# Every softmax from a copied score tile, the weights' clamp on GpSimd, and a planner with new costs for TensorE's forms

## The chip, the cores and the metric

The kernel runs on one core of a Trainium2 chip. The metric is the device time of one launch in microseconds, the median of several runs. Five engines share the work and run in their own order: PE (TensorE), DVE (VectorE), ACT (ScalarE), POOL (GpSimd) and SP, which issues the transfers.

## The reference, cut to what matters

Eight batches of attention (8 heads, 576 positions, head size 64) feed a mixing layer. In the attention a score counts only if it lies within tau of its row's largest:

```
scores = scale * q @ k.T
thresh = max(scores) - tau
attn = exp(where(scores >= thresh, scores, -1e9) - max(scores))
attn = attn / (sum(attn) + 1e-9)
x = attn @ v                       # heads side by side: 576 x 512 per batch
theta = x @ w_theta
y = w_tok_r @ (x * cos(theta)) + w_tok_i @ (x * sin(theta))
u = x + y
out = u + maximum(u @ w_ch, 0)
```

## The kernel before

**Precision.** fp32 products are made of three products of a high and a low part (names with 1 and 2, h and l). The weights are split once, in `convert`: four pieces of w_theta, nine of w_tok and four of w_ch, 17 in all. Each piece is loaded, passes ACT (absolute value, L407) and five DVE instructions (clamp L411, shift L418, then L425, L432, L436), ACT again, and three kinds of matmul on PE (L455 to L457).

**Attention.** Heads go in 32 pairs, four to a batch. A pair has five units: four of 128 query rows for both heads, and one for the last 64 rows of both together. So a pair has nine softmaxes of 128 x 576, called heads below and counted from the program's start (heads 1 to 9 are pair 1). A unit's scores (L552) fill a tile of four PSUM banks (two for the last unit) that always starts at bank 0 for the full units: one score tile is in flight at a time, and the next unit's scores wait until all readers of the last are done. Two ways of making the softmax stand in `unit`, chosen by `n < AT["pp"]`:
- *direct*: one DVE reduction over both heads (L567), the limits (L592), Exp on ACT from PSUM (L614), and a mask by DVE that reads the scores in PSUM again (L621);
- *copied*: for each head DVE copies the negated scores to SBUF and takes the extreme on the way (L583), then the limits (L600), Exp from the copy (L631), and a mask that reads the copy and the Exp, both in SBUF (L638).

Then PE turns the head round in blocks of 128 x 128 (L654, and L681 for the last keys), ACT copies the blocks to `a` (L660), and PE multiplies by the values (L710). A pair's row sums are turned on PE (L726), inverted on DVE (L731, L734), sent through DRAM to be spread, and multiplied in (L745). Before, the first five pairs (45 heads) are direct and the other 27 pairs copied.

**Mixing.** Each batch's `mixture` (L791 with w_theta or w_ch, L903 to turn, L932 with w_tok) is laid between the attention units of the next batch; batch 8's attention is the last, and the end of the program is mixing alone.

**TensorE's forms.** Scores of the full units use the array as two halves of 64 rows (64*128 in the rows below), the value products as two halves of 64 columns (128*64), everything else, transposes too, the whole array (128*128).

**The order.** `Plan.run` decides it before the program is built: a list scheduler with a cost for each operation (`c_ps`, `c_two`, `c_fast`, `c_pool`), due times (the table `AT`), and a lock that keeps some DVE and POOL operations apart. What it decides is then the fixed order of each engine. Its only knowledge of the forms is 0.1 added where they differ.

Of the kernel before, what the change touches and what calls it, by code (L numbers as in the profile page):

```python
# [32 lines left out]
AT = {  # L33
    "wait": 0.046, "margin": 0.0, "held": 1.639, "theta": 3.43, "theta_by": 2.2, "tok": 17.5, "tok_by": 0.87, "ch": 54.39,
    "ch_by": 3.55, "q": -4.49, "k": -10.75, "raw": -1.58, "v": -4.5, "m0": 8.15, "m1": 4.1, "score": -2.04, "nm": 0.6,
    "add": -4.86, "exp": -2.35, "mask": -0.34, "wrap": -0.65, "turn": 0.32, "copy": 1.0, "last": 0.06, "v0": 4.11, "v1": 13.27,
    "vcopy": -0.32, "div": 6.28, "rows": -1.77, "dmul": 0.16, "x": 0.95, "x_by": 0.51, "wm": -9.49, "ev": 2.19, "zst": 0.37,
    "sin": -0.88, "zm": -0.69, "zh": 0.09, "zl": -2.61, "y": -0.99, "u": 1.64, "fa": 0.68, "fa_by": 1.07, "ft": 0.17,
    "ft_by": 0.05, "pq": 28, "px": 2, "pu": 0, "pz": 6, "pk": 1, "ta": 4, "cut": 2, "pp": 5, "vm": 0, "m6": 0.15, "wp": 0,
    "wq": 0, "ua": 2, "ord": 0, "hang": 0, "n_rawq": 2, "n_rawk": 2, "n_q": 4, "n_rb": 2, "n_ang": 2, "n_xh": 4, "n_xl": 4,  # L40
    "n_wm": 3, "n_z": 3, "n_k": 4, "n_s2": 3, "n_nm": 4, "n_sc": 4, "n_a0": 1, "n_a1": 1, "n_zh4": 4, "n_zl4": 4, "n_zh1": 2,
    "n_zl1": 2, "n_xT": 7, "n_v": 2, "n_rows": 2, "n_rt": 1, "keep": -3.37,
}


# [61 lines left out]
class Plan:  # L107
# [39 lines left out]
    def run(self):  # L147
# [51 lines left out]
        while todo:  # L199
# [50 lines left out]
def tile_attn_moe(  # L250
# [11 lines left out]
    nc = tc.nc  # L262
# [118 lines left out]
    def convert(src, n, raw_cls, places, key, done, turn):  # L381
# [12 lines left out]
        def hb():  # L394
            return raw()[:, :n, 1]
# [13 lines left out]
        dve(
            c_fast(n),  # L410
            lambda: nc.vector.tensor_scalar(  # L411
                out=mb().bitcast(F32), in0=mb().bitcast(F32), scalar1=W_LEAST, scalar2=W_MOST, op0=ALU.max, op1=ALU.min
            ),
            key, (mag,), (mag,), lock=True,
        )
        dve(
# [118 lines left out]
    def unit(n, i):  # L535
# [69 lines left out]
        for j in heads:  # L605
# [5 lines left out]
            if n < AT["pp"]:  # L611
# [15 lines left out]
            else:  # L627
# [93 lines left out]
    def divide(n, key):  # L721
# [36 lines left out]
    def mixture(b, k0, k1):  # L758
# [134 lines left out]
        def flip(m, keys):  # L893
            z = zs[m]
            out = []
            for (c0, nb), key in zip(((0, 4), (4, 1), (5, 4)), keys):
# [8 lines left out]
                def tv(tp=tp, nb=nb):  # L905
# [181 lines left out]
```

## Time and profile before

| | |
|---|---|
| median of 3 runs | 1035.54 us (1034.57 to 1036.29) |
| the profiled execution | 1035.99 us, its span 1034.2 us |
| TensorE's mean granted clock | 0.992 |
| busy share of the span | PE 96%, DVE 77%, ACT 67%, POOL 23% |

The span is what the trace covers; 1.8 us lie around it. PE's share is an average of a first part of some 160 us, in which it often waits, and the rest, in which it hardly does. Busy times of matmuls overlap their neighbours'; how fast PE goes is read from the distance between starts.

### The profile page before, as it was taken

The page shows a single profiled execution, that of the slowest core. Times are in us where ns is not written, and L with a number is a line of the kernel's source. Part 1 is how long each engine was busy: PE and PEld are TensorE (multiplying, and loading weights), DVE is VectorE, ACT ScalarE, POOL GpSimd, SP SyncE. Part 2 cuts the span into 40 slices and gives each one's busy share as a digit, 9 for nine tenths or more (in the row PEclk, how much of TensorE's full clock was granted, in tenths as well). Part 3 has the DMA queues.
Part 4 walks back from the last instruction along what each step waited for, and adds up shares of the span by engine and source line. Part 5 has one row for each costly group of instructions (what it writes and reads, how often), then busy time and mean ns, then how long its engine had stood idle before and what let it go on. Part 6 is the DMA issues. An engine that isn't in the chain of part 4 may idle for free.

```text
span 1034.2 us, 21024 instructions
## 1 busy us (share of the span) xinstructions
PE 995.1 (96%) x8008; PEld 853.7 (83%) x8008; DVE 797.8 (77%) x1869; ACT 690.8 (67%) x1326; POOL 233.8 (23%) x257
## 2 busy tenths in 40 slices
PE   5888889999999999999999999999999999999998
PEld 3566578789898888898888888988888898888998
DVE  6998569987868778777877777887787869887462
ACT  6878577756786468765787558775687647864350
POOL 1002133111261123411252023511242112100100
PEclk9999899999999999999999999999999999999999
DMA  7651132234421143213430152212431142200601
GB/s 254 204 193 50 49 107 73 82 132 134 123 90 46 51 142 110 71 39 112 134 106 26 40 166 92 88 50 70 137 126 37 45 138 97 65 15 13 189 30 67
DMA packets 52308, 98.04 MB, mean 95 GB/s; under 512 B 12752, under 2 KB 21488, under 8 KB 52208
## 3 DMA queue, kind: packets, MB, share of 16 engines
q1 hardware_dynamic: 52208, 96.71, 29.1%
q8 instruction: 63, 1.03, 0.4%
q14 instruction: 37, 0.30, 0.1%
HBM read 82.90 MB, written 13.78 MB: 93 GB/s over the span
## 4 chain that ended last, share of the span: by engine, by line
PE 87%; DVE 6%; ACT 5%; issue 1%; DMA 1%; SPq 0%; ACTq 0%; DVEq 0%
PE banks_ps__66 L932 21%; PE banks_ps__66 L791 19%; PE banks_ps__66 L710 16%; PE banks_ps__66 L552 14%; PE banks_ps__66 L654 12%; PE banks_ps__66 L903 2%; PE banks_ps__66 L681 1%; DVE s L621 1%; DVE nm L567 1%; PE banks_ps__66 L455 1%; ACT a L660 1%; DVE zl L912 1%; DVE sc L583 1%; DMA z<-in_w_tok_dram 1%; PE banks_ps__66 L726 1%
## 5 line engine op out<-in xcount | busy, mean ns | idle before, releaser
L631 ACT ACTIVATE s<-sc,nm 128x576 f32<-128x576 f32 x243 | 186.5, 780 | 83.7 <-DVE sc L583 83.0
L638 DVE SCALAR_TENSOR_TENSOR s<-sc,nm,s 128x576 f32<-128x576 f32 x243 | 204.5, 869 | 39.0 <-ACT s L631 31.6
L583 DVE TENSOR_SCALAR_CACHE_REDUCE sc<-banks_ps__66 128x576 f32<-128x576 f32 x243 | 177.5, 746 | 66.2 <-PE banks_ps__66 L552 65.8
L660 ACT COPY a<-banks_ps__66 128x512 f32<-128x512 f32 x256 | 150.2, 591 | 94.0 <-PE banks_ps__66 L654 92.9
L654 PE MATMUL banks_ps__66<-ident,s 128*128 128x128 f32 x1152 | 173.4, 279 | 13.8 <-DVE s L621 12.9
L552 PE MATMUL banks_ps__66<-k,q 64*128 64x288 f32 (+1 forms) x1728 | 170.2, 311 | 7.7 <-ACT q L509 7.7
L710 PE MATMUL banks_ps__66<-a,v 128*64 128x320 f32 (+1 forms) x1280 | 171.8, 417 | 2.9 <-ACT a L668 1.7
L791 PE MATMUL banks_ps__66<-xh,wm 128*128 128x288 f32 x1024 | 171.6, 302 | 0.0
L932 PE MATMUL banks_ps__66<-wt_h,zh 128*128 128x288 f32 x576 | 166.1, 309 | 1.8 <-DVE zl L912 1.5
L654 PEld LDWEIGHTS banks_ps__66<-ident,s 128*128 128x128 f32 x1152 | 134.5, 142 | 40.2 <-DVE s L621 16.3
L368 POOL TENSOR_TENSOR k<-rawk,k 128x320 fp32r<-128x320 f32 x64 | 60.8, 972 | 460.5 <-issue 255.1
L932 PE MATMUL banks_ps__66<-wt_l,zh 128*128 128x288 f32 x576 | 162.4, 302 | 0.0
L552 PEld LDWEIGHTS banks_ps__66<-k,q 64*128 64x128 f32 (+1 forms) x1728 | 135.1, 188 | 32.0 <-issue 19.6
L791 PEld LDWEIGHTS banks_ps__66<-xh,wm 128*128 128x128 f32 x1024 | 144.8, 189 | 3.2 <-issue 2.2
L710 PEld LDWEIGHTS banks_ps__66<-a,v 128*64 128x64 f32 x1280 | 89.0, 139 | 67.4 <-issue 11.1
L932 PEld LDWEIGHTS banks_ps__66<-wt_h,zh 128*128 128x128 f32 x576 | 108.4, 188 | 4.9 <-DVE zl L912 3.2
L932 PEld LDWEIGHTS banks_ps__66<-wt_l,zh 128*128 128x128 f32 x576 | 108.6, 189 | 0.5 <-issue 0.5
L878 POOL TENSOR_TENSOR z<-z,xT 128x288 f32<-128x288 f32 x96 | 83.0, 905 | 94.5 <-ACT z L859 94.5
L791 PE MATMUL banks_ps__66<-xl,wm 128*128 128x288 f32 x512 | 98.3, 307 | 0.0
L932 PE MATMUL banks_ps__66<-wt_h,zl 128*128 128x288 f32 x576 | 97.5, 301 | 0.0
L932 PEld LDWEIGHTS banks_ps__66<-wt_h,zl 128*128 128x128 f32 x576 | 81.8, 188 | 2.2 <-issue 1.6
L791 PEld LDWEIGHTS banks_ps__66<-xl,wm 128*128 128x128 f32 x512 | 75.0, 189 | 2.0 <-issue 2.0
(79 smaller groups left out, 1249.3 us busy)
## 6 DMA issues: line engine op xcount, KB each, us to landing
wm<-wm_dram SPq DMA_DIRECT2D x64, 512.0 KB, 3.1
rawk<-in_kT_dram SPq DMA_DIRECT2D x32, 320.0 KB, 2.9
rawq<-in_qT_dram SPq DMA_DIRECT2D x32, 320.0 KB, 2.9
out_dram<-xT SPq DMA_DIRECT2D x31, 288.0 KB, 4.0
v<-in_vp_dram SPq DMA_DIRECT2D x32, 256.0 KB, 2.6
z<-in_w_tok_dram SPq DMA_DIRECT2D x9, 576.0 KB, 4.7
rb<-sums_dram SPq DMA_DIRECT2D x32, 144.0 KB, 3.1
wm_dram<-rb SPq DMA_DIRECT2D x16, 256.0 KB, 2.9
```

Of the source, the lines that this page charges most:

```text
L368: eng.tensor_tensor(out=out()[:, c0:c1], in0=in0()[:, c0:c1], in1=in1()[:, c0:c1], op=ALU.subtract)
L552: nc.tensor.matmul(ps()[:, 2 * j + h, :HS], q[a]()[r, i * P : (i + 1) * P], k[c]()[r, k0 : k0 + HS], start=(x == 0), stop=(x == 2))
L583: lambda j=j, sv=sv, sc=sc: nc.vector.tensor_scalar(out=view(sc()), in0=sv(), scalar1=-1.0, scalar2=None, op0=ALU.mult, op1=ALU.min, accum ...
L631: lambda j=j, sc=sc: nc.scalar.activation(out=s()[:, j], in_=sc(), func=AF.Exp, bias=nm()[:, j : j + 1], scale=-1.0),
L638: lambda j=j, sc=sc, total=total: nc.vector.scalar_tensor_tensor(out=s()[:, j], in0=sc(), scalar=nm()[:, 2 + j : 3 + j], in1=s()[:, j], op ...
L654: nc.tensor.transpose(out=tp()[:, c * P : (c + 1) * P], in_=s()[:, j, k0 : k0 + P], identity=ident)
L660: lambda j=j, tp=tp: nc.scalar.copy(out=a()[:, j:8:2, q0 : q0 + P], in_=tp().rearrange("p (c q) -> p c q", c=4)),
L710: nc.tensor.matmul(o()[64 * j : 64 * j + 64, :w], st, mv, start=(c == 0), stop=(c == 4))
L791: nc.tensor.matmul(ps[h]()[:, :HS], wm()[:, a, c, :], parts[c][bb]()[:, h * HS : (h + 1) * HS], start=first and n == 0, stop=final and n = ...
L878: eng.tensor_tensor(out=zi, in0=zi, in1=x[m]()[:, c0:c1], op=ALU.mult)
L903: nc.tensor.transpose(out=tp()[:, i * P : (i + 1) * P], in_=z()[:, c : c + P], identity=ident)
L932: nc.tensor.matmul(ps()[:, :HS], zz[c][lo]()[:, zz[c][2]], w[:, c, hs], start=(q + n == 0), stop=(q + n == len(work) - 1),)
```

## The change

- `pp` goes from 5 to 0: all 288 softmaxes take the copied way.
- The clamp of the first 13 weight pieces (`wc`: 13; w_theta and w_tok) goes from DVE to POOL, in two halves. The shift on DVE then waits for POOL.
- `SWITCH` gives the planner a cost for each pair of forms, with whole-array matmuls and transposes told apart; `favour` and `linger` make it pick, among PE's operations that are ready, one that is like the form in hand.
- The planner's costs of DVE's and POOL's operations are new (most DVE ones lower), and the due times in `AT` are another set.

No other arithmetic changes; the same 288 softmaxes, products and transfers are made.

```diff
-    "ft_by": 0.05, "pq": 28, "px": 2, "pu": 0, "pz": 6, "pk": 1, "ta": 4, "cut": 2, "pp": 5, "vm": 0, "m6": 0.15, "wp": 0,
+    "ft_by": 0.06, "pq": 28, "px": 2, "pu": 0, "pz": 6, "pk": 1, "ta": 4, "cut": 2, "pp": 0, "vm": 0, "m6": -0.89, "wp": 0,
...
+    "t_s": -0.13, "m_s": 1.51, "wc": 13,
...
+def SWITCH(old, new):
+    if old is None or (old in "mt" and new in "mt") or old == new:
+        return 0.0
+    if new == "t":
+        return 0.15
+    if old in "rv" and new in "rv":
+        return 0.145 if new == "v" else 0.196
+    return 0.198
...
+        def favour(o):
+            if o.mode == "v":
+                return AT["v_r"] if mode == "r" else AT["v_m"]
+            if mode not in ("r", "v") or o.mode == mode:
+                return 0.0
+            return AT["t_s"] if o.mode == "t" else AT["m_s"]
...
+            if e == PE:
+                t0 += AT["linger"]
+                return min(((o.key + favour(o), o.n), t, o) for t, o in got if t <= t0)[1:]
...
             if e == PE:
-                form = o.mode if o.mode in "vr" else "m"
-                if mode is not None and mode != form:
-                    occ += 0.1
-                mode = form
+                occ += SWITCH(mode, o.mode)
+                mode = o.mode
...
+        if turn < AT["wc"]:
+            for i in range(2):
+                gps(
+                    c_pool(n // 2), lambda i=i: clamp(nc.gpsimd, slice(n * i // 2, n * (i + 1) // 2)), key, ((mag, i),),
+                    ((mag, i),),
+                )
+        else:
+            dve(c_fast(n), lambda: clamp(nc.vector), key, (mag,), ((mag, [0, 1]),), lock=True)
```

What the planner makes of it is seen in the orders. First DVE in pair 4 (the fourth of the first batch), two units. Before (L567 reduction, L592 limits, L621 masks, L745 the row sums multiplied in, L368 a low part):

```order
L567 TENSOR_REDUCE nm<-banks_ps__66 128x2
L592 TENSOR_SCALAR nm<-nm,small 128x2
L621 SCALAR_TENSOR_TENSOR s_1027,rows<-banks_ps__66,nm,s_1027 128x576 x2
L567 TENSOR_REDUCE nm<-banks_ps__66 128x2
L592 TENSOR_SCALAR nm<-nm,small 128x2
L745 TENSOR_TENSOR xT<-xT,rb 128x576
L621 SCALAR_TENSOR_TENSOR s_1073,rows<-banks_ps__66,nm,s_1073 128x576 x2
L368 TENSOR_TENSOR xl<-xT,xh 128x576
```

The same two units of the changed kernel (L611 copies, L628 limits, L666 masks; L446, L464 steps of the weights' conversion, L773 row sums):

```order
L611 TENSOR_SCALAR sc,nm<-banks_ps__66 128x576 x2
L464 SCALAR_TENSOR_TENSOR xh<-z,xl 128x576
L628 TENSOR_SCALAR nm<-nm,small 128x2
L446 TENSOR_SCALAR xh<-xl 128x576
L666 SCALAR_TENSOR_TENSOR s_1063,rows<-sc,nm,s_1063 128x576 x2
L611 TENSOR_SCALAR sc,nm<-banks_ps__66 128x576 x2
L773 TENSOR_TENSOR xT<-xT,rb 128x576
L628 TENSOR_SCALAR nm<-nm,small 128x2
```

The reduction of two heads has become two copies, and steps of the weights' conversion, which were all done by then, stand between a unit's copies and its masks.

Second PE in a steady batch, around the value products of a pair's second half. Before (L552 scores, L710 values, L654 and L681 turn a head):

```order
L552 MATMUL banks_ps__66<-k,q 128x288 x12
L710 MATMUL banks_ps__66<-a_4761,v 64x320 x8
L710 MATMUL banks_ps__66<-a_4761,v_88 64x320 x2
L654 MATMUL banks_ps__66<-ident,s_5026 128x128 x8
L681 MATMUL banks_ps__66<-ident,s_5026 128x128
L552 MATMUL banks_ps__66<-k,q 128x288 x12
L654 MATMUL banks_ps__66<-ident,s_5081 128x128 x8
```

The changed kernel nearby (L580 scores, L738 values, L682 turns, L960 products with w_tok):

```order
L960 MATMUL banks_ps__66<-wt_h,zl_4994 128x288 x3
L580 MATMUL banks_ps__66<-k,q 128x288 x12
L738 MATMUL banks_ps__66<-a_5170,v 64x256 x8
L738 MATMUL banks_ps__66<-a_5170,v_90 64x256 x2
L580 MATMUL banks_ps__66<-k,q 128x288 x12
L682 MATMUL banks_ps__66<-ident,s_5223 128x128 x4
```

Value products now stand between two units' scores, without a visit to the whole array between them.

Third POOL at the start. Before (L308 zeroes, L368 low parts of k, q and x):

```order
L308 MEMSET v_90 128x128
masks.py:199 ISA
masks.py:199 AFFINE_SELECT ident<-ident 128x128
L368 TENSOR_TENSOR k<-rawk,k 128x320 x10
L368 TENSOR_TENSOR q<-rawq,q 128x320 x2
L368 TENSOR_TENSOR xl<-xT,xh 128x288 x4
```

Changed (L388 low parts, L432 the clamps):

```order
L388 TENSOR_TENSOR k<-rawk,k 128x320 x4
L432 TENSOR_SCALAR xl<-xl 128x256 x8
L432 TENSOR_SCALAR xl<-xl 128x288 x2
L388 TENSOR_TENSOR k<-rawk,k 128x320 x2
L432 TENSOR_SCALAR xl<-xl 128x288 x6
L388 TENSOR_TENSOR k<-rawk,k 128x320 x2
L432 TENSOR_SCALAR xl<-xl 128x288 x8
```

The halves of the clamps stand between the low parts of the next pairs' k, on an engine that had little to do there.

## Rows read from the trace of the kernel before

**Rows 1.** Busy us (instructions) by stretch: PE, PEld, DVE, ACT, POOL; PE's clock, DMA.

```profile
36.00:64.00 28.00, 23.60 (x172) 17.29 (x172) 27.72 (x57) 23.51 (x50) 1.90 (x2) 1.00 0.75 247
...
92.00:118.00 26.00, 19.64 (x155) 14.84 (x154) 17.36 (x32) 17.07 (x36) 6.49 (x9) 0.93 0.17 50
118.00:148.00 30.00, 27.63 (x205) 21.61 (x206) 20.52 (x40) 17.58 (x36) 3.60 (x5) 0.89 0.26 83
148.00:160.00 12.00, 9.32 (x57) 6.27 (x55) 6.21 (x13) 9.93 (x22) 7.93 (x10) 0.86 0.53 178
...
282.84:402.05 119.21, 119.09 (x990) 103.77 (x992) 93.33 (x229) 82.78 (x159) 33.88 (x36) 1.00 0.27 88
```

**Rows 2.** The waits of PE, 165 us to the end: total, times, longest.

```profile
PE banks_ps__66 L932 <- DVE zl L912: 1.5, 1, 1.5
PE banks_ps__66 L654 <- DVE s L638: 0.9, 1, 0.9
```

**Rows 3.** Instructions in order of time: direct units of pair 4, start and length.

```profile
97.32 1.06 PE L552 MATMUL banks_ps__66<-k,q 64*128 64x288 f32 x12
...
98.31 1.09 PE L654 MATMUL banks_ps__66<-ident,s 128*128 128x128 f32 x8
98.42 1.36 DVE L567 TENSOR_REDUCE nm<-banks_ps__66 128x2 f32<-128x1152 f32 x1 [1.34 <-PE banks_ps__66 L552]
...
99.23 0.27 PE L681 MATMUL banks_ps__66<-ident,s 128*128 128x128 f32 x1
...
101.63 0.81 PE L654 MATMUL banks_ps__66<-ident,s 128*128 128x128 f32 x4 [2.12 <-DVE s L621]
```

**Rows 4.** The same view: PE around one visit to the half-row form.

```profile
165.01 0.29 PE L932 MATMUL banks_ps__66<-wt_l,zh 128*128 128x288 f32 x1
165.24 1.07 PE L552 MATMUL banks_ps__66<-k,q 64*128 64x288 f32 x12
166.24 1.06 PE L932 MATMUL banks_ps__66<-wt_h,zl 128*128 128x288 f32 x6
167.14 0.60 PE L654 MATMUL banks_ps__66<-ident,s 128*128 128x128 f32 x4
```

**Rows 5.** Groups by line: count, busy us, mean ns, idle before and its releaser.

```profile
L638 DVE SCALAR_TENSOR_TENSOR s<-sc,nm,s 128x576 f32<-128x576 f32 x243 | 204.5, 869 | 39.0 <-ACT s L631 31.6 <-ACT a L660 0.5
L583 DVE TENSOR_SCALAR_CACHE_REDUCE sc<-banks_ps__66 128x576 f32<-128x576 f32 x243 | 177.5, 746 | 66.2 <-PE banks_ps__66 L552 65.8
L368 POOL TENSOR_TENSOR xl<-xT,xh 128x288 fp32r<-128x288 f32 x32 | 28.6, 928 | 180.7 <-ACT xh L752 180.7
L621 DVE SCALAR_TENSOR_TENSOR s<-banks_ps__66,nm,s 128x576 f32<-128x576 f32 x45 | 35.2, 813 | 5.2 <-ACT s L614 4.7
L567 DVE TENSOR_REDUCE nm<-banks_ps__66 128x2 f32<-128x1152 f32 x20 | 26.8, 1340 | 14.0 <-PE banks_ps__66 L552 13.9
L411 DVE TENSOR_SCALAR xl<-xl 128x576 f32<-128x576 f32 x9 | 4.0, 447 | 0.0
```

**Rows 6.** The same view as rows 3: two copies on DVE in a steady batch.

```profile
283.09 0.73 DVE L583 TENSOR_SCALAR_CACHE_REDUCE sc<-banks_ps__66 128x576 f32<-128x576 f32 x1
...
283.77 0.74 DVE L583 TENSOR_SCALAR_CACHE_REDUCE sc<-banks_ps__66 128x576 f32<-128x576 f32 x1
```

**Rows 7.** The same view: PE turns the row sums of pairs 3, 4 and 5.

```profile
91.82 0.27 PE L726 MATMUL banks_ps__66<-ident,rows 128*9 128x128 f32 x1
...
117.97 0.28 PE L726 MATMUL banks_ps__66<-ident,rows 128*9 128x128 f32 x1 [1.94 <-DVE s L621]
...
147.72 0.27 PE L726 MATMUL banks_ps__66<-ident,rows 128*9 128x128 f32 x1
```

**Rows 8.** The same view: two masks and the turn that needs the first, steady batch.

```profile
391.34 0.80 DVE L638 SCALAR_TENSOR_TENSOR s<-sc,nm,s 128x576 f32<-128x576 f32 x1
...
392.08 0.80 DVE L638 SCALAR_TENSOR_TENSOR s<-sc,nm,s 128x576 f32<-128x576 f32 x1
...
392.38 0.60 PE L654 MATMUL banks_ps__66<-ident,s 128*128 128x128 f32 x4
```

More of the change, by code (lines that the diff above doesn't have):

```diff
@@ L33 @@
 AT = {
[L34 to L38, printed above, removed]
-    "ft_by": 0.05, "pq": 28, "px": 2, "pu": 0, "pz": 6, "pk": 1, "ta": 4, "cut": 2, "pp": 5, "vm": 0, "m6": 0.15, "wp": 0,
+    "wait": 0.06, "margin": 0.0, "held": 1.639, "theta": 1.36, "theta_by": 2.2, "tok": 10.13, "tok_by": 4.15, "ch": 49.47,
+    "ch_by": 4.85, "q": -4.55, "k": -10.75, "raw": -1.33, "v": -1.4, "m0": 8.15, "m1": 3.84, "score": -2.12, "nm": 0.28,
+    "add": -2.06, "exp": -1.96, "mask": 0.65, "wrap": -0.41, "turn": 0.53, "copy": 0.97, "last": 0.49, "v0": 4.11, "v1": 13.27,
+    "vcopy": 3.92, "div": 3.45, "rows": -1.17, "dmul": -0.5, "x": 1.09, "x_by": 2.32, "wm": -9.49, "ev": 2.0, "zst": 0.88,
+    "sin": -0.64, "zm": 1.26, "zh": 1.71, "zl": -4.24, "y": -2.39, "u": 1.65, "fa": -0.63, "fa_by": 1.07, "ft": 0.17,
+    "ft_by": 0.06, "pq": 28, "px": 2, "pu": 0, "pz": 6, "pk": 1, "ta": 4, "cut": 2, "pp": 0, "vm": 0, "m6": -0.89, "wp": 0,
     "wq": 0, "ua": 2, "ord": 0, "hang": 0, "n_rawq": 2, "n_rawk": 2, "n_q": 4, "n_rb": 2, "n_ang": 2, "n_xh": 4, "n_xl": 4,
     "n_wm": 3, "n_z": 3, "n_k": 4, "n_s2": 3, "n_nm": 4, "n_sc": 4, "n_a0": 1, "n_a1": 1, "n_zh4": 4, "n_zl4": 4, "n_zh1": 2,
-    "n_zl1": 2, "n_xT": 7, "n_v": 2, "n_rows": 2, "n_rt": 1, "keep": -3.37,
-}
+    "n_zl1": 2, "n_xT": 7, "n_v": 2, "n_rows": 2, "n_rt": 1, "keep": -3.85, "linger": 0.03, "v_r": -0.13, "v_m": 0.12,
+    "t_s": -0.13, "m_s": 1.51, "wc": 13,
+}
+def SWITCH(old, new):
[6 more added lines that the diff above has]
+    return 0.198
 def ON_POOL(what, n, j):
@@ L183, in choose @@
                 return None
-            t0 = min(t for t, _ in got) + AT["wait"]
+            t0 = min(t for t, _ in got)
+            if e == PE:
+                t0 += AT["linger"]
+                return min(((o.key + favour(o), o.n), t, o) for t, o in got if t <= t0)[1:]
+            t0 += AT["wait"]
             return min(((o.key + AT["held"] * held_up(o, t, AT["margin"]), o.n), t, o) for t, o in got if t <= t0)[1:]
@@ L333, in c_ps @@
     def c_ps(n):
-        return n / 960 + 0.085
+        return n / 960 + 0.07
     def c_two(n):
-        return n / 960 + 0.14
+        return n / 960 + 0.067
     def c_fast(n):
-        return n / 1920 + 0.05
+        return n / 1920 + 0.061
     def c_act(n, ps=False, ptr=False):
@@ L406, in convert, with clamp @@
         act(
-            c_act(n), lambda: nc.scalar.activation(out=mb().bitcast(F32), in_=hb().bitcast(F32), func=AF.Abs), key, (raw,), (mag,)
-        )
[L409 to L415, printed above, removed]
+            c_act(n), lambda: nc.scalar.activation(out=mb().bitcast(F32), in_=hb().bitcast(F32), func=AF.Abs), key, (raw,),
+            ((mag, [0, 1]),),
+        )
+        def clamp(eng, r=slice(0, n)):
+            eng.tensor_scalar(
+                out=mb().bitcast(F32)[:, r], in0=mb().bitcast(F32)[:, r], scalar1=W_LEAST, scalar2=W_MOST, op0=ALU.max, op1=ALU.min
+            )
[4 more added lines that the diff above has]
+                    ((mag, i),),
+                )
+        else:
+            dve(c_fast(n), lambda: clamp(nc.vector), key, (mag,), ((mag, [0, 1]),), lock=True)
         dve(
@@ L565, in unit @@
             dve(
-                c_ps(S * len(heads)),
+                S * len(heads) / 960 + 0.015,
                 lambda: nc.vector.tensor_reduce(
@@ L733, in divide @@
         )
-        dve(0.25, lambda: nc.vector.reciprocal(out=rt(), in_=rt()), key + AT["rows"], (rt,), (rt,))
+        dve(0.85, lambda: nc.vector.reciprocal(out=rt(), in_=rt()), key + AT["rows"], (rt,), (rt,))
         load(lambda: nc.sync.dma_start(sums_dram[n], rt()), key + AT["keep"], (rt,), (kept,), 5)
```

12 lines of the change are left out of this document (6 added, 6 removed).

## The prediction

> **What bounds the kernel now.** I read the busy times by stretch first, then PE's waits, then the instructions in order of time in the stretches that these point to. The program has two parts. From some 165 us on PE is the bound: in the stretch of one batch it is busy 119.09 of 119.21 us [rows 1], and from 165 us to the end it waits only 2.4 us in all [rows 2]. Work that any other engine saves there is worth nothing; work that PE saves is worth its full length. Before 165 us it is the other way round: between 36 and 64 us DVE is busy 27.72 of 28 us and PE 23.60, so DVE is the bound. Between 92 and 148 us neither is: DVE falls to 17.36 of 26 and 20.52 of 30 [rows 1]. There the direct softmax is a chain with one score tile: scores at 97.32, reduction from 98.42, Exp, two masks, the turn at 101.63 with a wait of 2.12 us for the mask [rows 3], and only then the next scores.
>
> I count this first part in one way for both kernels. For a head, take the work that stands ahead of it in PE's order (instructions times the distance between their starts) and the work that stands ahead of its mask in DVE's order. The turn cannot start before DVE's work plus DVE's own delay, so
>
> PE's lost time = DVE's lead over PE in work + DVE's delay.
>
> The distances: a copy 0.68 [rows 6], a mask 0.74 [rows 8], a reduction of two heads 1.27 (its 1340 ns [rows 5] less the 0.07 by which neighbours overlap), a 288-column product 0.134 and a turned block 0.11 (six products from 166.24 to 167.14 with 0.1 of a form's change [rows 4]; eight blocks from 98.31 to 99.23 with some of a change [rows 3]), the rest likewise. Before, the lead is largest at head 30: DVE 83.7, PE 67.6, lead 16.1. The turn came at 101.63 [rows 3], so DVE's delay was 17.9 and PE had lost 34.0. At the row sums of pairs 3, 4 and 5 (91.82, 117.97, 147.72 [rows 7]; DVE's work 76.9, 92.4, 111.4; PE's work 60.9, 78.4, 102.1) DVE's delay is 14.9, 25.6 and 36.3, and PE's loss 30.9, 39.6 and 45.6. So up to pair 3 DVE hardly idles: about 10.5 of its delay is the time to the first mask, and 4.4 came in three pairs. In the next 56 us the chain adds 21. Between 148 and 160 us PE is busy 9.32 of 12 at a clock of 0.86 [rows 1], which adds 2.7 and 1.7: its loss is then 50, and it hardly grows after that.
>
> **The change part by part.**
>
> *Copied softmax for pairs 1 to 5.* On DVE a full unit now takes two copies, limits and two masks, 2 x 0.68 + 0.13 + 2 x 0.74 = 2.97, for 1.27 + 0.13 + 2 x 0.74 = 2.88: 22.5 units, +2 us. What it gives is the score tile: its last reader is the second copy, not the second mask, so the next scores can run under limits and masks, and conversion steps now stand between (the first piece of order). A round on the score tile becomes PE's scores 1.0 [rows 4], some 0.3 to the first copy and 1.4 of copies, 2.7 us, under DVE's 2.97: DVE binds, not the chain. ACT, busy 23.51 of 28 [rows 1], does the same number of Exps.
>
> *Clamp to POOL.* 13 clamps leave DVE: 447 ns less 0.07, so 0.37 each [rows 5], 4.8 us. POOL gets 26 halves; its price for a tensor_scalar is in no row; the nearest is 928 ns for 288 columns [rows 5], so 26 x 0.93 = 24 us of an engine that was busy 1.90 of 28 [rows 1], spread over some 100 us. The Trainium skill ("GPSIMD Engine Reference", Engine selection) says that with one input GpSimd is roughly at line rate; at an estimated 0.3 us a half these would be 8 us, which no run here shows. The new wait is DVE's: each shift stands behind POOL's two halves, with the next copies and masks queued behind it. Hidden, it costs 0; at worst a whole clamp, 1.86. I take 0, since ACT's absolute value and POOL come well ahead in the order.
>
> *The port.* Masks in the first part used to read PSUM and SBUF; now they read two tiles in SBUF. Masks of the second kind take 869 ns, of the first 813 [rows 5]: 56 ns each on average, 45 masks, 2.5 us. With POOL busier than in a steady batch I take 4 for all DVE instructions; bounds 0 and 24 (each half delays DVE by its length). [...]
>
> *The first part's sum.* In the changed orders DVE's work ahead of head 36, the end of pair 4, is 87.6 for 92.4, and its largest lead over PE is 14.0, at head 40 (95.6 and 81.6); by head 50 it is 4.0. Its delay there: 10.5 to the first mask, 1.5 a pair as in the first three (4.4 pairs, 6.5), and 4 for the port: 21. PE's loss is 14 + 21 = 35, for 50: **15 us**. Bounds: the delay stays at the 14.9 of pair 3 (loss 29, gain 21), or it grows as before in pairs 4 and 5 (31 at head 40, between the 25.6 and 36.3; loss 45, gain 5). I take a value near the lower one, because what made it grow was the chain.
>
> *Forms.* One visit of the half-row form: from 165.01 to 167.14 lie one product, six pairs of half products and six products, 13 x 0.134 = 1.74; 2.13 passed, so two changes cost 0.39, 0.195 each [rows 4]. In the orders I count changes of form (transposes are whole-array): 321 before, 294 after; 39 and 36 in a steady batch. Those into scores or whole-array products fall from 179 to 147, those into transposes or values rise from 142 to 147. At 0.195 for all it is 27 x 0.195 = 5.3; if the second kind costs only 0.1 it is 5.7. I take **5.5**, nearly all of it on the path, since PE is the bound for most of it. That the change does not do this is ruled out: the order is fixed.
>
> *Cover in the steady batches.* A head's turn needs copy, Exp and mask behind its scores; in PE's order other work covers that. Before, the thinnest cover of a two-head unit was 4.1 us, and the turn started 0.24 after its mask's end (391.34 + 0.80 to 392.38) [rows 8]: 3.86 of it was used. In the new order four such heads a batch have 3.4 to 3.5. Bounds: 0 (elsewhere DVE and ACT are free and it takes less) and 4 x 0.4 = 1.6 a batch; I take 0.3, six batches, **2 us lost**.
>
> *The rest.* The number of transfers is the same. In SP's queue the second k and the first weight piece now go ahead of pair 1's values, which PE needs only after two units are turned; hidden. The program's end is mixing in the same order in both: 0.
>
> Sum: 1035.99 - 15 - 5.5 + 2 = 1017.5 for an execution like the profiled one, which is 0.45 above the median of the runs: **1017 us**.
>
> **The rivals.**
> - *The first part stays a chain* (ACT's queue or PE's order takes the score tile's place): gain 5 there, 5.3 of forms, 2 lost: 1027. For it: DVE, ACT and PE are all near 80% or more between 36 and 64 us. Against: DVE is busy 99% there [rows 1].
> - *Thin covers wait in every batch*: 1.6 x 6 = 10 lost for 2: 1025. Together with the first it would be near 1034.
> - *POOL holds DVE* (the other side): if each clamp half holds DVE 0.93, by the port or because the shift waits for it, DVE's delay rises by 24 for the 4 taken: 1037. It decides from about 0.9 us a half. For it: both engines are queues, and DVE is the bound there. Against: 56 ns a mask in batches in which POOL is busy 33.88 of 119.21 us [rows 1].
> - *The delay stays at pair 3's*: gain 21 there: 1011.
>
> **Numbers.** The forecast's own case (loss 29 to 39 in the first part, 1010 to 1022) 0.62, *delay stays* at its lower end and below 0.08, chain 0.15, covers 0.08, POOL 0.07. About 0.2%, 2 us, is what a measurement can tell from none. Faster 0.91, same 0.04, slower 0.05, the last two from POOL and from chain and covers together. Range 1007 to 1029: it leaves out POOL, part of the chain case and a loss under 27.
>
> **What would show it.** PE's last wait of the first part near 140 us, where before it is near 160; DVE busy over 90% from 92 to 118 us; scores starting right behind the second copy; a steady batch at 118.5 to 118.8 for 119.21. I am wrong if DVE's shifts wait for POOL, if masks in the first part take over 0.9 us, or if a steady batch has waits of PE for masks.

## The result

| | before | changed |
|---|---|---|
| median of 4 runs each | 1035.91 us (1034.57 to 1036.68) | 1018.00 us (1017.49 to 1021.77) |
| ratio | | 0.9836, 95% interval 0.981 to 0.9862 |
| profiled execution, its span | 1035.99, 1034.2 us | 1018.16, 1016.4 us |

The forecast was 1017, with 1007 to 1029 as its range. In the changed kernel the scores are L580, the copy L611, the limits L628, Exp L659, the mask L666, the turn L682, the row sums' turn L754 and the clamp L432.

Busy us by stretch of the changed kernel (columns as in [rows 1]; the last stretch is one batch):

```profile
36.00:64.00 28.00, 25.59 (x184) 18.43 (x184) 27.65 (x67) 25.64 (x53) 12.93 (x11) 1.00 0.73 235
92.00:118.00 26.00, 24.33 (x184) 18.07 (x183) 25.29 (x62) 21.41 (x45) 7.84 (x8) 0.93 0.19 57
118.00:148.00 30.00, 29.06 (x242) 24.41 (x241) 22.42 (x56) 24.43 (x50) 9.99 (x12) 1.00 0.28 95
148.00:160.00 12.00, 12.00 (x96) 10.73 (x95) 11.12 (x29) 8.26 (x17) 0.00 (x0) 1.00 0.41 132
362.08:481.15 119.07, 118.61 (x990) 103.64 (x992) 93.37 (x228) 81.80 (x159) 34.45 (x37) 1.00 0.28 89
```

Against [rows 1], DVE (third) is now full from 92 to 118 us too, 25.29 of 26 for 17.36, and PE is at 29.06 of 30 from 118 on, where it had 27.63: the first part ends near 118 us and not near 160. PE's waits of the changed kernel, from 92 to 165 us:

```profile
PE banks_ps__66 L580 <- DVE sc L611: 1.4, 2, 0.9
PE banks_ps__66 L931 <- ACT a L688: 0.9, 1, 0.9
PE banks_ps__66 L754 <- DVE s L666: 0.3, 1, 0.3
```

The turn of a head waits for no mask there any more; what is left is scores that wait for a copy, and single waits of the mixing (L931) and of the row sums' turn. The instructions in order of time, for [rows 3]:

```profile
106.73 0.40 PE L580 MATMUL banks_ps__66<-k,q 64*128 64x288 f32 x1 [0.89 <-DVE sc L611]
106.80 0.73 DVE L611 TENSOR_SCALAR_CACHE_REDUCE sc<-banks_ps__66 128x576 f32<-128x576 f32 x1
...
107.60 1.61 PE L580 MATMUL banks_ps__66<-k,q 64*128 64x288 f32 x11 [0.47 <-DVE sc L611]
...
109.04 0.80 DVE L666 SCALAR_TENSOR_TENSOR s<-sc,nm,s 128x576 f32<-128x576 f32 x1
```

The first scores of the next unit run beside the second copy, the rest 0.07 us behind its end (106.80 + 0.73), 1.4 us before the first of the unit's masks has begun: the tile is free at the copy.

Where the 17.8 us of span come from is read at two marks that have the same work ahead of them on PE in both kernels: the turns of the row sums of pairs 12 and 28. In the kernel before:

```profile
359.35 0.27 PE L726 MATMUL banks_ps__66<-ident,rows 128*9 128x128 f32 x1
...
836.27 0.27 PE L726 MATMUL banks_ps__66<-ident,rows 128*9 128x128 f32 x1
```

and in the changed one:

```profile
343.54 0.27 PE L754 MATMUL banks_ps__66<-ident,rows 128*9 128x128 f32 x1
...
819.74 0.27 PE L754 MATMUL banks_ps__66<-ident,rows 128*9 128x128 f32 x1
```

So 15.8 us were won by pair 12, 0.7 in the four batches from there (119.23 a batch, now 119.05), and 1.3 from pair 28 to the end. The changes of form, counted in the traces, are 122 and now 110 up to pair 12, 156 and 144 in the four batches, 43 and 40 after.

### The profile page after: what moved, and what is told of

It is laid out like the page before. It is cut to its first block, busy times and chain, and to the rows that moved or that the text cites. A ratio compares the mean times of both kernels' runs of the same rounds, so it can differ in the third digit from the quotient of the medians.

```text
span 1016.4 us, 21090 instructions
## 1 busy us (share of the span) xinstructions
PE 988.6 (97%) x8008; PEld 852.8 (84%) x8008; DVE 796.1 (78%) x1921; ACT 687.0 (68%) x1326; POOL 275.6 (27%) x283
## 4 chain that ended last, share of the span: by engine, by line
PE 76%; DVE 13%; ACT 8%; issue 2%; DMA 1%; SPq 0%; DVEq 0%; ACTq 0%
PE banks_ps__66 L960 21%; PE banks_ps__66 L819 14%; PE banks_ps__66 L738 13%; PE banks_ps__66 L580 12%; PE banks_ps__66 L682 11%; DVE s L666 4%; DVE sc L611 3%; ACT s L659 2%; PE banks_ps__66 L931 2%; PE banks_ps__66 L709 1%; DVE ang L852 1%; DVE z L862 1%; ACT z L887 1%; ACT L884 1%; PE banks_ps__66 L483 1%
## 5 line engine op out<-in xcount | busy, mean ns | idle before, releaser
L666 DVE SCALAR_TENSOR_TENSOR s<-sc,nm,s 128x576 f32<-128x576 f32 x288 | 238.1, 853 | 36.2 <-ACT s L659 28.8
L659 ACT ACTIVATE s<-sc,nm 128x576 f32<-128x576 f32 x288 | 214.1, 775 | 71.5 <-DVE sc L611 70.3
L611 DVE TENSOR_SCALAR_CACHE_REDUCE sc<-banks_ps__66 128x576 f32<-128x576 f32 x288 | 209.8, 751 | 55.2 <-PE banks_ps__66 L580 55.1
L580 PE MATMUL banks_ps__66<-k,q 64*128 64x288 f32 (+1 forms) x1728 | 176.1, 313 | 13.6 <-ACT q L537 7.7
L819 PE MATMUL banks_ps__66<-xh,wm 128*128 128x288 f32 x1024 | 174.8, 304 | 0.0
L580 PEld LDWEIGHTS banks_ps__66<-k,q 64*128 64x128 f32 (+1 forms) x1728 | 137.9, 188 | 43.8 <-issue 20.2
L682 PE MATMUL banks_ps__66<-ident,s 128*128 128x128 f32 x1152 | 172.5, 278 | 1.3 <-DVE s L666 1.1
L738 PE MATMUL banks_ps__66<-a,v 128*64 128x320 f32 (+1 forms) x1280 | 168.7, 412 | 1.2 <-ACT a L696 1.2
L960 PE MATMUL banks_ps__66<-wt_h,zh 128*128 128x288 f32 x576 | 163.1, 304 | 1.6 <-DVE zl L940 1.6
L960 PE MATMUL banks_ps__66<-wt_l,zh 128*128 128x288 f32 x576 | 161.9, 303 | 0.0
L388 POOL TENSOR_TENSOR k<-rawk,k 128x320 fp32r<-128x320 f32 x64 | 66.2, 1055 | 347.1 <-issue 209.0
L682 PEld LDWEIGHTS banks_ps__66<-ident,s 128*128 128x128 f32 x1152 | 133.6, 142 | 22.1 <-issue 11.6
L738 PEld LDWEIGHTS banks_ps__66<-a,v 128*64 128x64 f32 x1280 | 88.6, 137 | 63.6 <-issue 8.4
L960 PEld LDWEIGHTS banks_ps__66<-wt_h,zh 128*128 128x128 f32 x576 | 108.4, 188 | 2.3 <-DVE zl L940 1.8
L960 PEld LDWEIGHTS banks_ps__66<-wt_l,zh 128*128 128x128 f32 x576 | 108.5, 188 | 0.0
L960 PE MATMUL banks_ps__66<-wt_h,zl 128*128 128x288 f32 x576 | 99.3, 302 | 0.0
L819 PE MATMUL banks_ps__66<-xl,wm 128*128 128x288 f32 x512 | 93.8, 300 | 0.0
L960 PEld LDWEIGHTS banks_ps__66<-wt_h,zl 128*128 128x128 f32 x576 | 81.7, 188 | 0.2 <-issue 0.2
L972 DVE TENSOR_TENSOR xT<-banks_ps__66,xT 128x288 f32<-128x288 f32 x64 | 29.0, 453 | 63.0 <-PE banks_ps__66 L960 62.9
```

Of the source, the lines that this page charges most:

```text
L388: eng.tensor_tensor(out=out()[:, c0:c1], in0=in0()[:, c0:c1], in1=in1()[:, c0:c1], op=ALU.subtract)
L580: nc.tensor.matmul(ps()[:, 2 * j + h, :HS], q[a]()[r, i * P : (i + 1) * P], k[c]()[r, k0 : k0 + HS], start=(x == 0), stop=(x == 2))
L611: lambda j=j, sv=sv, sc=sc: nc.vector.tensor_scalar(out=view(sc()), in0=sv(), scalar1=-1.0, scalar2=None, op0=ALU.mult, op1=ALU.min, accum ...
L659: lambda j=j, sc=sc: nc.scalar.activation(out=s()[:, j], in_=sc(), func=AF.Exp, bias=nm()[:, j : j + 1], scale=-1.0),
L682: nc.tensor.transpose(out=tp()[:, c * P : (c + 1) * P], in_=s()[:, j, k0 : k0 + P], identity=ident)
L738: nc.tensor.matmul(o()[64 * j : 64 * j + 64, :w], st, mv, start=(c == 0), stop=(c == 4))
```

## The experiments

Each was timed in 3 rounds (the last in 5) beside runs of the kernel before on the same chip. Rows with different medians of the kernel before (1034.28 to 1036.09 us) come from different chips, and a difference of two medians across them is good to some 2 us. "Mark" is the turn of pair 12's row sums in its profile; e9, e10 and e11 have four more products ahead of it, e10 another twenty value products.

| kernel | median us | before beside it | ratio (95% interval) | mark us |
|---|---|---|---|---|
| changed | 1018.00 | 1035.91 | 0.9836 (0.981 to 0.9862) | 343.54 |
| e1_direct | 1044.94 | 1034.28 | 1.0099 (1.0083 to 1.0116) | 368.56 |
| e2_copied | 1037.04 | 1034.28 | 1.0025 (1.0014 to 1.0036) | 360.22 |
| e4_no_forms | 1025.18 | 1034.28 | 0.9911 (0.9895 to 0.9927) | 346.79 |
| e5_tile_held | 1053.85 | 1034.28 | 1.0181 (1.0161 to 1.02) | 380.05 |
| e3_clamp_back | 1020.88 | 1035.26 | 0.987 (0.9838 to 0.9902) | 345.64 |
| e6_no_clamp | 1017.47 | 1035.26 | 0.9846 (0.9806 to 0.9886) | 340.05 |
| e7_whole | 1045.12 | 1035.26 | 1.0103 (1.0071 to 1.0134) | 347.65 |
| e7_half | 1024.39 | 1035.26 | 0.9908 (0.9875 to 0.994) | 344.26 |
| e9_copied_due | 1029.63 | 1034.66 | 0.996 (0.994 to 0.9981) | 350.65 |
| e10_old_due | 1051.80 | 1034.66 | 1.0176 (1.0149 to 1.0203) | 358.23 |
| e11_direct_due | 1040.62 | 1034.66 | 1.0084 (1.0054 to 1.0114) | 364.43 |
| e12_replanned | 1014.22 | 1036.09 | 0.98 (0.9787 to 0.9814) | 339.99 |

**Direct again, and the copied form that holds its tile.** Theory: what the copied softmax gives is the early release of the score tile. e1_direct is the changed kernel with one number other:

```diff
-"cut": 2, "pp": 0, "vm": 0,
+"cut": 2, "pp": 5, "vm": 0,
```

> The changed kernel with the first five pairs' softmaxes taken directly from the score tile again; clamp on POOL, form costs and order rules as changed. 308 changes of form for 294, all the 14 more in the first part (36 stay in a steady batch). Theory (the copied softmax frees the score tile, which ends the chain): PE's loss in the first part goes back up by about 13, and 14 changes x 0.195 = 2.7 come on top: 13 to 16 us over the changed kernel, some 1032. Rival (the first part's gain came from the clamp, the due times or the order): within 4 us of the changed kernel.

e5_tile_held keeps the copied form, but names the score tile among what the mask of pairs 1 to 5 reads, so that the next scores are planned behind the mask:

```diff
-t0 + j + AT["mask"], (sc, (nm, 2), (s, j)), ((s, j), (pr.rows, total)), lock=True,
+t0 + j + AT["mask"], (sc, (nm, 2), (s, j), *([(ps, j)] if n < 5 else [])), ((s, j), (pr.rows, total)), lock=True,
```

> The changed kernel, but the planner holds the score tile of the first five pairs until the mask, as it was with direct softmaxes, while the operations are those of the copied form (the copies, the masks on SBUF tiles). 307 changes of form for 294. It tells the tile's release from the rest of the copied form. Theory (what the copied form gives is the earlier release): 10 to 15 us over the changed kernel, 1028 to 1033. Rival (shorter operations or the due times give the gain): within 4 us.

Measured: 27 and 36 us over the changed kernel, both slower than before. The rival is out, and the sizes are two to three times the expected ones. PE's waits of e1_direct from 36 to 165 us:

```profile
PE banks_ps__66 L682 <- DVE s L649: 11.5, 6, 2.5
PE banks_ps__66 L754 <- DVE s L649: 6.7, 4, 2.4
```

and of e5_tile_held, the same stretch:

```profile
PE banks_ps__66 L682 <- DVE s L666: 13.2, 8, 2.6
PE banks_ps__66 L754 <- DVE s L666: 6.5, 3, 2.7
```

The changed kernel has 0.9 and 1.8 us of these. One of the eight, in e5_tile_held's order of time:

```profile
107.83 0.56 PE L580 MATMUL banks_ps__66<-k,q 64*128 64x288 f32 x6
...
108.43 0.76 DVE L611 TENSOR_SCALAR_CACHE_REDUCE sc<-banks_ps__66 128x576 f32<-128x576 f32 x1 [4.07 <-PE banks_ps__66 L580]
...
110.79 0.82 DVE L666 SCALAR_TENSOR_TENSOR s<-sc,nm,s 128x576 f32<-128x576 f32 x1
...
111.67 0.66 PE L682 MATMUL banks_ps__66<-ident,s 128*128 128x128 f32 x4 [2.57 <-DVE s L666]
```

It is the round of [rows 3], with the same operations as in the changed kernel: DVE has nothing for 4.07 us until the scores are there, and PE nothing for 2.57 until the mask is. Holding the tile is enough to bring the chain back, whatever form the softmax has. Part of the size is TensorE's clock: the mean granted share from 92 to 118 us, 0.93 in the changed kernel, is 0.80 in both. The stretch in e1_direct:

```profile
92.00:118.00 26.00, 20.66 (x139) 14.47 (x139) 14.36 (x27) 13.59 (x28) 5.42 (x7) 0.80 0.17 49
```

and in e5_tile_held:

```profile
92.00:118.00 26.00, 18.63 (x117) 13.57 (x117) 16.70 (x42) 14.51 (x30) 4.46 (x6) 0.80 0.17 49
```

0.80 is a mix of the two levels, 1.2 and 2.4 GHz. Idle time in the same stretch does not by itself tell the clock: the kernel before has 0.93 there with PE busy for 19.64 us of 26 [rows 1]. Another part may be that the due times fit the other form, below; the sizes were not taken apart.

**The copied form by itself, and the due times.** The same theory says that the kernel before gains from the copied form alone. e2_copied is the kernel before with `"pp": 0`.

```diff
-"cut": 2, "pp": 5, "vm": 0,
+"cut": 2, "pp": 0, "vm": 0,
```

> The kernel before with one number changed: no pair is direct, all softmaxes are copied; clamp on DVE and the old form rule stay. 323 changes of form for 321, 39 to 40 in a steady batch. Theory (the score tile): 10 to 15 us less than before, about 1022 to 1026. Rival (the copied form alone loads DVE more and gains only with the clamp gone from DVE): within 4 us of before, or slower.

Measured: 1.0025, so 2.8 us slower, with the mark 0.9 us later than before. This expectation of the theory fell. PE's waits of e2_copied, 84 to 165 us:

```profile
PE banks_ps__66 L791 <- ACT xh L752: 4.3, 1, 4.3
PE banks_ps__66 L654 <- DVE sc L583: 4.0, 1, 4.0
PE banks_ps__66 L654 <- DVE s L638: 3.9, 2, 3.4
```

The chain of two-microsecond waits is gone, but three single waits stand in its place, each for one operation that comes late: an input of the mixing, a copy and a mask. The order is planned from the due times, and these may have had another form in view. Three more kernels ask that. e9_copied_due is the kernel before, copied, with the changed kernel's due times:

```diff
+AT.update({'wait': 0.06, 'theta': 1.36, 'tok': 10.13, 'tok_by': 4.15, 'ch': 49.47, 'ch_by': 4.85, 'q': -4.55, 'raw': -1.33, 'v': -1.4, 'm1': 3.84, 'score': -2.12, 'nm': 0.28, 'add': -2.06, 'exp': -1.96, 'mask': 0.65, 'wrap': -0.41, 'turn': 0.53, 'copy': 0.97, 'last': 0.49, 'vcopy': 3.92, 'div': 3.45, 'rows': -1.17, 'dmul': -0.5, 'x': 1.09, 'x_by': 2.32, 'ev': 2.0, 'zst': 0.88, 'sin': -0.64, 'zm': 1.26, 'zh': 1.71, 'zl': -4.24, 'y': -2.39, 'u': 1.65, 'fa': -0.63, 'ft_by': 0.06, 'pp': 0, 'm6': -0.89, 'keep': -3.85})
```

> The kernel before with no pair direct and, of the changed kernel, its due times; clamp on DVE, the old costs and the old rule on forms stay (321 changes). It asks why the copied form alone gave nothing (the kernel before with copied softmaxes took 1.0025 times as long). Theory (the copied form ends the chain, but its gain shows only under due times that fit it; the old ones leave three long waits of PE for a copy, a mixing input and a mask): the changed kernel's time plus some 7 for the forms and 0 to 3 for the clamp, 1022 to 1030. Rival (forms, clamp and costs are what makes the copied form pay): within 4 us of before, or over it.

e11_direct_due is the same line without its `'pp': 0`, so that the first five pairs stay direct:

```diff
-'ft_by': 0.06, 'pp': 0, 'm6': -0.89,
+'ft_by': 0.06, 'm6': -0.89,
```

> The kernel before, five pairs direct as there, with the due times of the changed kernel: the fourth corner of direct or copied by old or new due times. Theory (with direct softmaxes the turn waits for the mask whatever the due times): no faster than before, 1035 to 1055. Rival (the new due times are the gain by themselves): 1018 to 1027.

e10_old_due is the changed kernel with the due times of before, the reverse of that line (some of it):

```diff
+AT.update({'wait': 0.046, 'theta': 3.43,
...
+'mask': -0.34, 'wrap': -0.65, 'turn': 0.32, 'copy': 1.0, 'last': 0.06, 'vcopy': -0.32, 'div': 6.28,
...
```

> The changed kernel (copied, clamp on POOL, new costs and rule on forms) with the due times of before. Theory (due times that do not fit leave long waits in the first part): 12 us or more over the changed kernel, 1030 to 1050, with waits of PE of 2 us and more before 165 us. Rival (the due times matter little): within 4 us of the changed kernel.

With the kernel before's costs, rule on forms and clamp, the square is: direct with old due times 1; direct with new ones 1.0084; copied with old ones 1.0025; copied with new ones 0.996. Neither half pays alone, the two together give 4 to 5 us (2 to 6 by the interval), and some 9 us at the mark. Of the theory's expectations e9_copied_due, at its upper edge, and e11_direct_due are in their ranges, e10_old_due is 2 us beyond its own; what fell is that the copied form would do it by itself. The rival of e9_copied_due, within 4 us of before, is not excluded by that interval: the larger part of the 17.9 us came only with the costs, the clamp and the rule on forms. e10_old_due loses much of its time elsewhere than expected: its mark comes 14.7 us late (with some 2.6 us more work ahead of it), and 18 more are lost after that, half of it in waits of later batches for ACT (PE's waits from 165 us on):

```profile
PE banks_ps__66 L710 <- ACT a L689: 9.7, 3, 3.2
```

So the old due times under the new costs and the new rule on forms are a misfit of their own, and the 33.8 us are no price of the due times in the first part.

**The rule on forms.** e4_no_forms puts the old rule and its 0.1 back into the changed kernel:

```diff
-            t0 = min(t for t, _ in got)
-            if e == PE:
-                t0 += AT["linger"]
-                return min(((o.key + favour(o), o.n), t, o) for t, o in got if t <= t0)[1:]
-            t0 += AT["wait"]
+            t0 = min(t for t, _ in got) + AT["wait"]
...
-                occ += SWITCH(mode, o.mode)
-                mode = o.mode
+                form = o.mode if o.mode in "vr" else "m"
+                if mode is not None and mode != form:
+                    occ += 0.1
+                mode = form
```

> The changed kernel with the old planning of forms: 0.1 a change by the old classes, and no favour for the form that PE is in. 324 changes for 294, 40 in a steady batch for 36. Theory (each change costs about 0.195 on PE, which is the bound from 165 us on): 30 x 0.195 = 5.9, less the 2 to 3 that thin covers may give back: 3 to 6 us over the changed kernel, and a steady batch 0.4 to 0.8 longer. Rival (grouping forms is worth nothing, since what it saves comes back as waits): within 1.5 us.

Measured: 7.2 us over the changed kernel, a little above the range. Its mark is 3.25 us late, the four batches from there to pair 28 take 2.0 us more, the end 2.2. The rival is out: grouping is worth several us. A batch takes 119.55 for 119.07 (pair 12 to pair 16), 0.48 for four changes, 0.12 each. That is a net figure, as the same batch of e4_no_forms shows:

```profile
346.79:466.34 119.55, 119.52 (x990) 103.94 (x989) 94.16 (x229) 82.46 (x159) 34.53 (x37) 1.00 0.28 88
```

PE is idle for 0.03 us here and for 0.46 of the changed kernel's batch (119.07 less 118.61, above): busy time falls by 0.91 with the four changes, 0.23 each, and half of it comes back as waits. Since 0.12 is not the 0.195 of the prediction, the price was asked for by itself with twins:

```diff
+                if x == 1 and i < 4 and 8 <= n < 28:
+                    nc.tensor.matmul(ps()[:, 0, 300:308], one[0:P], minus[0:P, 0:8], start=False, stop=False)
```

in e7_whole; in e7_half the operands are `one[0:64]` and `minus[0:64, 0:8]`. The added products go into unused columns.

> The changed kernel with one more 8-column product, of the whole array, in the middle of the half-row score products of each full unit of pairs 8 to 27, into unused columns: 80 products, each two more changes of form, 160 in all. It is compared with its twin, whose added product has half rows. Theory (0.195 a change): 31 us longer than the twin. Rival (0.1, as the old planner counted): 16. If changes are free: 0.

> The twin: the same 80 added 8-column products with half rows, so that no form changes. Only their own length, some 80 x 0.03 to 0.1 us: 2 to 8 us over the changed kernel.

Measured: the twins differ by 20.7 us, 0.13 a change, between the theory and its rival and nearer to the rival. In order of time, e7_whole:

```profile
226.76 0.53 PE L582 MATMUL banks_ps__66<-k,q 64*128 64x288 f32 x4
227.22 0.27 PE L577 MATMUL banks_ps__66<-minus,one 128*128 128x8 f32 x1
227.42 0.79 PE L582 MATMUL banks_ps__66<-k,q 64*128 64x288 f32 x8
```

and e7_half:

```profile
227.57 0.55 PE L582 MATMUL banks_ps__66<-k,q 64*128 64x288 f32 x4
227.94 0.16 PE L577 MATMUL banks_ps__66<-minus,one 64*128 64x8 f32 x1
227.96 0.77 PE L582 MATMUL banks_ps__66<-k,q 64*128 64x288 f32 x8
```

From the first scores to the last group 0.66 us pass with the changes and 0.39 without: 0.27 a visit. A batch (pairs 12 to 16, marks 347.65 and 472.14, 344.26 and 464.49) takes 124.49 and 120.23 us, 4.26 for 32 changes, 0.133 each. But the twin has a cost of its own, though it changes no form: its batch is 1.16 us longer than the changed kernel's (120.23 for 119.07), 0.07 for each added product of 8 columns. If the added product costs as much in either form, a change costs 0.133. If the whole-array one costs nothing but its two changes, the 5.42 us by which e7_whole's batch is over the changed kernel's make 0.17 a change. So the twins put the price between 0.13 and 0.17 and do not fix it.

Nor is the visit in [rows 4] an odd one. By the same sum, the thirteen visits of that shape (a product, twelve half-row products, six products) in the kernel before from 160 us on cost 0.36 to 0.38 us each, and the 31 in e4_no_forms 0.36 to 0.39, against 0.27 between the twins. How much of the difference is the twin's own 0.07 stays open.

**The clamp.** Both kernels keep the changed kernel's order. e3_clamp_back issues the halves on DVE, e6_no_clamp leaves out the clamp of the first 13 weight pieces:

```diff
-c_pool(n // 2), lambda i=i: clamp(nc.gpsimd, slice(n * i // 2, n * (i + 1) // 2)), key, ((mag, i),),
+c_pool(n // 2), lambda i=i: clamp(nc.vector, slice(n * i // 2, n * (i + 1) // 2)), key, ((mag, i),),
```

```diff
-c_pool(n // 2), lambda i=i: clamp(nc.gpsimd, slice(n * i // 2, n * (i + 1) // 2)), key, ((mag, i),),
+c_pool(n // 2), lambda: None, key, ((mag, i),),
```

> The changed kernel with the same order on every engine, but the 26 clamp halves run on DVE, at their places, instead of POOL. DVE gets some 26 x 0.24 = 6 us more of work in the first part, where it is the bound; POOL and the shared port are relieved. Theory (clamp on POOL is hidden, port about 4 in all): DVE +6 - 4: +1 to +5 us. Rival (POOL's halves hold DVE): 3 us or more faster than the changed kernel.

> The changed kernel in the same order, with the clamp of the first 13 weight pieces left out (the rest of the conversion stays). It measures the whole price of the clamp on POOL, wait and port together. Theory (hidden, port up to 4): 0 to 4 us faster. Rival (POOL's halves hold DVE): 6 us or more faster.

Measured: 2.9 us slower and 0.5 us faster by the medians, 3.5 and 1.0 us slower by the ratios, with intervals that overlap the changed kernel's: neither difference is settled. The marks, 2.1 late and 3.5 early, are single profiles, and both fit the theory; but up to 1.8 us of the 3.5 can be the clock, which from 92 to 118 us was 1.00 in e6_no_clamp and 0.93 in the changed kernel:

```profile
92.00:118.00 26.00, 23.56 (x192) 17.16 (x191) 25.76 (x64) 22.96 (x48) 7.95 (x8) 1.00 0.16 50
```

The rival is out in both: 3 us faster with the clamp on DVE, 6 us and more without it. The halves on POOL in the changed kernel (groups by line, 8 to 165 us):

```profile
L432 POOL TENSOR_SCALAR xl<-xl 128x288 f32<-128x288 f32 x18 | 25.2, 1413 | 23.6 <-ACT xl L427 23.6
...
L432 POOL TENSOR_SCALAR xl<-xl 128x256 f32<-128x256 f32 x8 | 10.6, 1342 | 2.3 <-ACT xl L427 2.3
```

They take 35.8 us in all, where the prediction put 24.

**A plan with the twins' price.** e12_replanned gives every change 0.133 and moves 15 numbers of `AT` (14 in the expectation) for that price, the search going by the planner's own costs:

```diff
+AT.update({'wait': 0.058, 'copy': 0.725, 'mask': 0.945, 'linger': 0.017, 'last': 0.421, 'ft': 0.157, 'theta_by': 2.174, 'm6': -0.715, 'rows': -0.829, 'sin': -0.834, 'tok_by': 4.02, 'tok': 10.029, 'ch': 49.803, 'keep': -4.643, 'ch_by': 5.015})
...
-    if new == "t":
-        return 0.15
-    if old in "rv" and new in "rv":
-        return 0.145 if new == "v" else 0.196
-    return 0.198
+    return 0.133
```

> The changed kernel planned once more with 0.133 a change of form, the price that the twins with added products gave, in place of 0.15 to 0.2, and with 14 due times and cushions moved a little for that price. 295 changes of form, 36 in a steady batch, as before. If prices and due times of this size matter: 1 to 3 us faster than the changed kernel, 1015 to 1017. If the plan is already flat here, as small planning differences are lost in the noise of the first part: within 2 us of it, either way.

Measured: 1014.22 us, 3.8 under the changed kernel, a little more than expected; the intervals of the two ratios overlap by a hair (0.981 to 0.9814). It has the lowest median here. Its mark is 3.55 us early, and a batch takes 118.80 for 119.05. The batch from pair 12 on, and PE's waits from 165 us on:

```profile
339.99:458.81 118.82, 118.65 (x990) 103.66 (x989) 93.48 (x229) 81.96 (x159) 34.11 (x37) 1.00 0.29 89
```

```profile
PE banks_ps__66 L957 <- DVE zl L937: 1.6, 1, 1.6
PE banks_ps__66 L679 <- DVE s L663: 0.9, 5, 0.2
```

PE is as busy as in the changed kernel's batch (118.61), with 36 changes of form in both; what went is waiting, from 0.46 to 0.17 us. The changed kernel waits 2.6 us at the turn of the row sums from 165 us on (below), this one not there, but 0.2 us at a time at the turn of a head. So in the batches the gain is a better fit of the order to the masks. Whether the price or one of the 15 numbers brought it was not separated.

## Why the prediction was right

**The first part: 15 forecast, some 14 measured.** Of the 15.8 us at the mark, 12 changes of form at 0.13 to 0.17 are 1.6 to 2.0; 13.8 to 14.2 are PE's lost time. The points named ahead came so: DVE over 90% from 92 to 118 us (97%), scores behind the second copy, masks at 852 ns on the mean, under the 0.9 that would have spoken against it; the last wait of over 0.5 us in the first part ends before 144 us. What the prediction gave as the reason, the tile, is shown by e5_tile_held, but it is not the whole reason: e2_copied shows that the tile is worth nothing while the due times plan for another form. The prediction took the changed order as it stood, so its number held both without telling them apart.

In steps by the mark: before 359.35, with copied form and new due times 350.65 (and some 0.5 us more work ahead of the mark), with new costs and the clamp on POOL 346.79 (that is e4_no_forms), with the rule on forms 343.54. The first two steps, which hold the copied form and the clamp, are 12.6 of the 15.8 us; the rule on forms is 3.25, of which its eight changes up to there are 1.0 to 1.4. The new costs were tried in no run by themselves.

**TensorE's clock is part of the gain.** From 92 to 160 us the kernel before was granted 0.93, 0.89 and 0.86 in the three stretches of [rows 1], the changed kernel 0.93, 1.00 and 1.00. And the time of a kernel goes with the mean clock of the run: the kernel before took 1037.57, 1037.99 and 1038.40 us in its three runs at 0.990, and 1030.23, 1030.34 and 1031.14 in those at 0.998; the changed kernel took 1021.77 at 0.990, and 1017.49 and 1018.16 at 0.998. At the same clock the gain is 13 to 16 us; the other 2 to 5 of the 17.9, an estimate from these runs, come with the clock. The prediction put the clock at 1.7 us, from 148 to 160; any more of it stands in its 21 us between pairs 3 and 5, which it gave to the chain alone.

**Forms: 5.5 forecast, 3.6 to 4.6 measured.** The count of 27 was right. The price was 0.195 a change, from a visit in [rows 4]; the twins put it at 0.13 to 0.17, and PE's busy time in a batch fell from 119.09 [rows 1] to 118.61 with three changes less, 0.16 each. The term came out 1 to 2 us smaller. The steady batch does not show that: the 118.5 to 118.8 named for it does not follow from the prediction's own terms, by which 119.21 less three times 0.195 and plus 0.3 for covers is 118.9; 119.05 came.

**Thin covers: 2 lost forecast, about that measured.** PE's idle time in a batch rose from 0.12 us [rows 1] to 0.46, 0.34 a batch or 2.0 in six. (With the twins' 0.133, three changes are 0.40 of which a batch gained 0.18, and 0.22 came back, 1.3 in six.) The waits of PE in the changed kernel from 165 us on, for [rows 2]:

```profile
PE banks_ps__66 L754 <- DVE s L666: 2.6, 6, 0.5
PE banks_ps__66 L960 <- DVE zl L940: 1.6, 1, 1.6
PE banks_ps__66 L709 <- ACT q L537: 0.7, 1, 0.7
```

One wait a batch, at the turn of the row sums and not at the four thin heads: the size was right, the place was not. The prediction named waits of PE for masks in a steady batch as a sign of being wrong, and here they are, 0.46 us a batch; they cost no more than it had allowed for covers. The rival with 10 us is out.

**The clamp: no wait, port 4 of lengthening forecast.** DVE waits for POOL nowhere in the first part. The rival needed each half to hold DVE, and they took 1.4 us each, not 0.93, without doing so. What the halves cost is that some of DVE's instructions beside them are longer. The changed kernel, in order of time:

```profile
10.02 2.09 POOL L432 TENSOR_SCALAR xl<-xl 128x256 f32<-128x256 f32 x2
11.02 0.45 DVE L628 TENSOR_SCALAR nm<-nm,small 128x2 f32<-128x2 f32 x1
...
12.46 2.70 POOL L432 TENSOR_SCALAR xl<-xl 128x256 f32<-128x256 f32 x2 [0.34 <-ACT xl L427]
12.67 0.95 DVE L666 SCALAR_TENSOR_TENSOR s<-sc,nm,s 128x576 f32<-128x576 f32 x1
...
14.84 0.60 DVE L460 TENSOR_SCALAR xl<-xh 128x512 uint32<-128x512 uint32 x1
```

and the same instructions in e6_no_clamp:

```profile
10.94 0.23 DVE L628 TENSOR_SCALAR nm<-nm,small 128x2 f32<-128x2 f32 x1
...
12.37 0.81 DVE L666 SCALAR_TENSOR_TENSOR s<-sc,nm,s 128x576 f32<-128x576 f32 x1
...
14.39 0.42 DVE L460 TENSOR_SCALAR xl<-xh 128x512 uint32<-128x512 uint32 x1
```

By e6_no_clamp's mark all of it is at most 3.5 us, and less if part of that is the clock; 4 was forecast. The rule of the Trainium skill ("SBUF — State Buffer", Who interferes with whom) that DVE and GpSimd share a pair of ports to SBUF, on which DVE instructions with two SBUF inputs, and tensor_scalar in some of its modes, can exclude GpSimd's, agrees with these rows in sign. The masks, which the prediction had in view, take 852 ns on the mean from 8 to 148 us and 845 in e6_no_clamp: they were hardly touched, and of the rows above the two tensor_scalar instructions (L628, L460) grew more than the mask.

**The sum.** At 0.133 a change it is 14.2 + 3.6 - 0.9 (covers to pair 28) + 0.9 (the end, forecast at 0, left unexplained), at 0.17 it is 13.8 + 4.6 - 1.3 + 0.8; either is, up to rounding, the 17.8 us of the two spans, and the forecast was 18.5. By either price the first part and the forms gave 2 to 3 us less than forecast, and the rest 1.5 to 2 more. That 1017 lies so near to 1018 is in part luck.

## What to carry to other kernels

Freeing a buffer earlier is worth only what the order does with it: test the form with the old order and the new order apart, since here each alone lost time and both together won. A price that enters a count of dozens is worth a pair of twins; but look at what the twin without the change costs, and at the idle time that comes and goes, before the difference is called the price: here the price stays a range. Compare runs at the same clock, or say what the clock brings. And planning again can be worth as much as a term: e12_replanned won its batches by waits that went, with as many changes of form as the changed kernel.

## What the runs showed that was not expected

A clamp of 128 x 288 values took POOL 1413 ns on the mean, where the nearest row of before, a subtraction of the same width, was 928 [rows 5], and where DVE in e3_clamp_back took 294 ns on the mean for the same eighteen. The Trainium skill ("GPSIMD Engine Reference", Engine selection), by which one-input work on GpSimd is roughly at line rate, does not hold for it here: it is nearly five times DVE's. It cost little because DVE waited for it nowhere.
